# Weight exponents moved by a factor in ScalarE, the clamp replaced by a row sum, and loads chained by issue

## The chip, the cores and the metric

The kernel runs on one core of one Trainium2 chip. The metric is device time in microseconds (us), the median of several runs. A core has a matrix engine (PE), a vector engine (DVE), a scalar engine (ACT), a general engine (POOL) and a queue processor (SP) that here issues nearly all DMAs.

## The reference

A linear attention with decay (4 batches, 8 heads, 768 steps, 48 channels a head) feeds two feed-forward layers (3072 tokens, width 384, inner width 2048). The weights w_in and w_out arrive as 64-bit floats and are converted to 32 bits on the chip.

```
for t in range(S):
    cur = einsum('bhd,bhe->bhde', u[None] * kt, vt)
    y[:, :, t] = einsum('bhd,bhde->bhe', rt, state + cur)
    state = wt[..., None] * state + einsum('bhd,bhe->bhde', kt, vt)
# twice, with weights of their own:
h = maximum(x @ w_in, 0);  x = (h * h) @ w_out
```

## The kernel before

**Tiling.** The attention is cut into 24 tiles of 128 tokens. Each layer walks over blocks of tokens: 512, 256, 256, 512, 512, 512, 512 in the first layer and 512, 512, 512, 512, 512, 256, 256 in the second. Within a block there are 16 slots, one for each chunk of 128 inner channels. A slot is nine matmuls into `h` (L675), relu, square, a rounded copy `gh` and a rest `gl` (L682 to L700), and the matmuls into `acc` (L718). Each fp32 factor is split into a high and a low part (`whi`, `wlo`, `xh`, `xl`, `gh`, `gl`), and three products replace one. From the first matmul of a layer's first block on, chunk f of the weights has to be ready for slot f.

**The weights.** A chunk of weights is loaded as 64-bit numbers (`raw`, 786 KB), and `chunk_ops` (L433) makes fp32 of it in the class `ToFloat32`: `magnitude` on ACT takes the absolute value of the high word (L407). Then four DVE operations on 128x768 numbers follow: `clamp` (L410), `shift` (L413), `top` (L416) and `tail` (L419). ACT copies the result to `whi` (L451) and DVE subtracts that to get `wlo` (L454). There are three `raw` buffers and two `c` buffers, so chunk k+3 can be loaded only when `tail` of chunk k is done. In the first layer the sixteen conversions run beside the ramp and the first block.

**An attention tile.** `wkr` (decays, keys, queries by channel) is loaded by L181, `vn` and `sv` (values) by L192 and L195. DVE runs two scans, G and F (L216, L222), forms a product `rk` (L233) and scales keys and queries by the scans (L246). ACT squares the scans into a sum that is tested at the end (L250). PE, ACT and POOL make scores, masks and states; DVE carries the state (`Sp` L323, `Sn` L333), adds up `ys` (L363) and makes `xl` (L379) beside ACT's `xh`. The first block needs the x of tiles 0 to 3. Until then PE runs matmuls on `ident` only to stay busy (L624).

**What sets the order.** Nothing is scheduled at run time. `Order` keeps a model of time at build: each operation has an engine, a cost from the table `COST`, what it needs, the buffers it takes and gives back, and a due time. `run` picks the operation that can start first, with ties by due time, and writes it out. The engines then execute in that order and wait on semaphores. For a load the model's result counts as there when modelled transfers have been served, plus `LATENCY` (2 us). In the kernel before each load of a kind (`w` for wkr, `v`, `rk`, `raw`) needs the previous one of its kind, that is, its landing in the model. These needs exist in the model alone; on the chip SP issues in the written order, waits for buffers, and each of eight DMA semaphores is reused in turn, so a ninth load waits until the first has landed.

Of the kernel before, what the change touches and what calls it, by code (L numbers as in the profile page):

```python
# [19 lines left out]
T = 128  # L20
# [16 lines left out]
HIGH_WORD_MIN, HIGH_WORD_MAX = 2.0 ** -15, 2.0 ** 16 * (1.875 - 2.0 ** -23)  # L37
RAW_BUFS = 3
# [9 lines left out]
            pe_y=1.14, pe_x=0.45, magnitude=0.91, clamp=0.55, shift=0.56, top=0.96, tail=0.96, hi=0.83, lo=0.96, issue=0.4, warm=0.3)  # L48
# [6 lines left out]
class Order:  # L55
# [37 lines left out]
    def run(self):  # L93
        while self.missing:
# [21 lines left out]
            if gives is not None:  # L116
                self.at[gives], self.by[gives] = end, "DMA" if moves else engine
                for o in self.waiting.pop(gives, ()):
                    o[10] -= 1
                    if not o[10]:  # L120
                        self.ready.append(o)


class Attn:
# [4 lines left out]
    def __init__(self, ctx, tc, wkr, nat, u, ub, ps):  # L129
# [11 lines left out]
        self.chk = cp.tile([QR, NTILE], F32, name="chk")  # L141
# [19 lines left out]
    def tile_ops(self, order, i, due, xdst):  # L161
# [22 lines left out]
        for n, (lo, hi) in enumerate(zip(cuts, cuts[1:])):  # L184
            add("SP", C_["issue"], lambda lo=lo, hi=hi: load_wkr(lo, hi), "w" if n == 0 else f"w{n}", [f"w{n - 1}" if n > 1 else "w"] if n else [("w", i - 1)] if i else [],
# [11 lines left out]
        add("SP", 3 * C_["issue"], load_v, "v", [("v", i - 1)] if i else [], -0.5, take=[("v", i)], moves=8 * T * DM)  # L197

        if not by_pe:
# [4 lines left out]
            add("SP", C_["issue"], load_rk, "rk", [("rk", i - 1) if i > SUMMED_BY_PE else ("rkT", i - 1)], -0.5, take=[("rk", i)], moves=8 * T * DM)  # L204
# [45 lines left out]
        add("ACT", C_["square"], lambda: nc.scalar.activation(out=t["GF"][:, :, 1:], in_=t["GF"][:, :, 1:], func=AF.Square, accum_out=self.chk[:, i:i + 1]),  # L250
# [131 lines left out]
    def out_of_range(self):  # L382
# [39 lines left out]
class Weights:  # L422
# [10 lines left out]
    def chunk_ops(self, order, k, due):  # L433
# [11 lines left out]
        def magnitude():  # L445
            t["conv"] = ToFloat32(nc, t["raw"], self.tmp_p.tile([128, 2 * DM], I32, tag="c", name="c"))
# [158 lines left out]
def chunked(ctx, tc, wkr, nat, u, ub, w1, w2, out):  # L605
# [53 lines left out]
    for k in range(2 * KF):  # L659
        W.chunk_ops(order, k, at[number[k // KF, 0, k % KF]] - 12)  # L660
# [194 lines left out]
```

## Time and profile before

| what | us |
|---|---|
| median of 3 runs (lowest, highest) | 968.42 (965.11, 970.42) |
| profiled execution: its own time | 969.43 |
| profiled execution: span in the trace | 967.6 |
| PE busy | 944.3 (98%) |
| DVE busy | 541.0 (56%) |
| ACT busy | 470.1 (49%) |
| POOL busy | 103.4 (11%) |

Busy PE is not useful PE: matmuls are pipelined, their ends are modelled, and the matmuls on `ident` count as busy. The useful work of the two layers starts with the first L675. A share over the whole span is a mean over a ramp, a first block with conversions, and a long rest, so the stretches are read apart.

### The profile page before, as it was taken

The numbers are of one execution on the slowest core, as the hardware profiler recorded it, in microseconds if no ns is written. First come the engines' busy times: TensorE is split into PE (matmuls) and PEld (weight loads), VectorE is DVE, ScalarE is ACT, GpSimd is POOL, SyncE is SP. The second block draws the span as 40 slices with busy tenths as digits, with TensorE's granted clock in tenths as the row PEclk, the third lists the DMA queues.
The fourth block names the chain that finished last, engine by engine and source line by source line (L and its number), as shares of the span: only waits on it lengthen the run. The fifth ranks groups of instructions, "written<-read, shape, count | busy, mean of one in ns | idle before, by whom it ended". The sixth has DMA issues, their size and how long they took to land.

```text
span 967.6 us, 16982 instructions
## 1 busy us (share of the span) xinstructions
PE 944.3 (98%) x6836; PEld 829.2 (86%) x6836; DVE 541.0 (56%) x946; ACT 470.1 (49%) x875; POOL 103.4 (11%) x122
## 2 busy tenths in 40 slices
PE   9899989999999999999999999999999999999996
PEld 9787678999887878878888889999999999999996
DVE  5889898778756465563337899432322322223332
ACT  3577757566645545464444565432433423333442
POOL 1301113044403123030100000000000000000000
PEclk9799999999999999999999999999999999999999
DMA  8355424154313322131024353110200100100000
GB/s 261 117 160 193 148 78 124 34 141 124 108 33 97 114 70 91 33 96 45 1 73 157 130 179 105 35 43 1 65 1 1 60 1 1 50 1 14 31 18 20
DMA packets 28119, 73.83 MB, mean 76 GB/s; under 512 B 3616, under 2 KB 15264, under 8 KB 28032
## 3 DMA queue, kind: packets, MB, share of 16 engines
q1 hardware_dynamic: 27904, 72.66, 24.2%
q8 instruction: 55, 0.90, 0.4%
q14 instruction: 32, 0.26, 0.1%
q10 hardware_dynamic: 128, 0.00, 0.0%
HBM read 63.21 MB, written 9.44 MB: 75 GB/s over the span
## 4 chain that ended last, share of the span: by engine, by line
PE 89%; DVE 7%; issue 2%; ACT 1%; DMA 1%; POOL 0%; DVEq 0%; POOLq 0%; ACTq 0%
PE acc L718 40%; PE h L675 39%; PE h L624 3%; PE ab L289 2%; PE ab L358 2%; DVE gl L700 1%; PE ab L314 1%; PE ab L258 1%; DVE c L416 1%; DVE Sp L323 1%; PE ab L368 1%; DVE gh L694 1%; DMA wkr<-in_wkr_dram 1%; DVE wlo L454 0%; DVE c L419 0%
## 5 line engine op out<-in xcount | busy, mean ns | idle before, releaser
L682 ACT ACTIVATE gf<-h 128x512 f32<-128x512 f32 (+1 forms) x224 | 120.0, 536 | 350.5 <-PE h L675 345.0
L694 DVE CAST gh<-gf 128x512 fp32r<-128x512 f32 (+1 forms) x208 | 87.3, 420 | 325.8 <-PE acc L718 294.1
L675 PE MATMUL h<-xh,whi 128*128 128x512 f32 (+1 forms) x672 | 245.2, 365 | 0.0
L675 PE MATMUL h<-xh,wlo 128*128 128x512 f32 (+1 forms) x672 | 243.0, 362 | 0.2 <-DVE wlo L454 0.2
L675 PE MATMUL h<-xl,whi 128*128 128x512 f32 (+1 forms) x672 | 242.9, 362 | 0.1
L700 DVE TENSOR_TENSOR gl<-gf,gh 128x512 fp32r<-128x512 f32 (+1 forms) x224 | 144.3, 644 | 15.6 <-ACT gh L694 0.8
L675 PEld LDWEIGHTS h<-xh,wlo 128*128 128x128 f32 x672 | 126.5, 188 | 20.2 <-DVE wlo L454 1.0
L675 PEld LDWEIGHTS h<-xl,whi 128*128 128x128 f32 x672 | 126.6, 188 | 17.5 <-DVE xl L379 0.7
L675 PEld LDWEIGHTS h<-xh,whi 128*128 128x128 f32 x672 | 126.6, 188 | 17.4
L687 ACT ACTIVATE gf<-gf 128x512 f32<-128x512 f32 (+1 forms) x224 | 128.1, 572 | 6.8
L718 PE MATMUL acc<-whi,gl 128*128 128x384 f32 x384 | 129.4, 337 | 0.0
L718 PE MATMUL acc<-whi,gh 128*128 128x384 f32 x384 | 129.3, 337 | 0.0
L718 PE MATMUL acc<-wlo,gh 128*128 128x384 f32 x384 | 128.9, 336 | 0.0
L718 PE MATMUL acc<-gl,whi 128*128 128x512 f32 (+1 forms) x336 | 122.3, 364 | 6.1 <-DVE gl L700 5.3
L718 PE MATMUL acc<-gh,whi 128*128 128x512 f32 (+1 forms) x336 | 124.9, 372 | 0.6 <-DVE gh L694 0.5
L718 PE MATMUL acc<-gh,wlo 128*128 128x512 f32 (+1 forms) x336 | 121.5, 361 | 0.0
L718 PEld LDWEIGHTS acc<-gl,whi 128*128 128x128 f32 x336 | 63.7, 190 | 18.0 <-DVE gl L700 8.2
L718 PEld LDWEIGHTS acc<-whi,gh 128*128 128x128 f32 x384 | 72.3, 188 | 3.5
L718 PEld LDWEIGHTS acc<-wlo,gh 128*128 128x128 f32 x384 | 72.2, 188 | 3.4
L718 PEld LDWEIGHTS acc<-gh,whi 128*128 128x128 f32 x336 | 63.6, 189 | 11.3 <-DVE gh L694 0.7
L718 PEld LDWEIGHTS acc<-whi,gl 128*128 128x128 f32 x384 | 72.0, 188 | 0.0
L718 PEld LDWEIGHTS acc<-gh,wlo 128*128 128x128 f32 x336 | 63.7, 190 | 9.4
(64 smaller groups left out, 946.7 us busy)
## 6 DMA issues: line engine op xcount, KB each, us to landing
raw<-in_w_dram SPq DMA_DIRECT2D x32, 768.0 KB, 4.4
wkr<-in_wkr_dram SPq DMA_DIRECT2D x23, 675.9 KB, 6.7
rk<-in_nat_dram SPq DMA_DIRECT2D x18, 384.0 KB, 5.3
vn<-in_nat_dram SPq DMA_DIRECT2D x24, 192.0 KB, 2.6
sv<-in_nat_dram SPq DMA_DIRECT2D x48, 96.0 KB, 2.6
out_dram<-o SPq DMA_DIRECT2D x24, 192.0 KB, 1.9
x<-o SPq DMA_DIRECT2D x15, 256.0 KB, 2.2
xr<-x SPq DMA_DIRECT2D x12, 256.0 KB, 2.6
```

The source lines that it names most:

```text
L258: nc.tensor.transpose(out=kbv[:, p, :], in_=kS[:, 2 * p:2 * p + 2, :].rearrange("q c t -> q (c t)"), identity=self.ident[0:QR, 0:QR])
L289: nc.tensor.matmul(out=t["sc"][other[a], n, :], lhsT=kS[rows, n, :], rhs=rT[rows, n, :], start=True, stop=True)
L314: nc.tensor.matmul(out=t["U"][c][q, p, :], lhsT=t["ksT"][rows, p, q], rhs=t["vn"][rows, 2 * p + a, :], start=True, stop=True)
L323: nc.vector.tensor_tensor(out=t["Sp"], in0=self.Sc[b], in1=ae, op=ALU.mult)
L358: nc.tensor.matmul(out=y[64 * c:64 * c + 64, D * h:D * h + D], lhsT=t["rs"][rows, a, 2 * p + c, :], rhs=t["sv"][rows, a, 2 * p + c, :], st ...
L624: nc.tensor.matmul(out=t[:, 0:128], lhsT=A.ident, rhs=A.ident, start=True, stop=True)
L675: nc.tensor.matmul(out=h[:, 0:N], lhsT=a[:, cs], rhs=b[:, kk, 0:N], start=n == 0, stop=n == 8)
L682: nc.scalar.activation(out=g[:, 0:N], in_=hs.pop((l, j, f))[:, 0:N], func=AF.Relu)
L687: nc.scalar.activation(out=g[:, 0:N], in_=g[:, 0:N], func=AF.Square)
L694: copy(out=gh[:, 0:N], in_=g[:, 0:N])
L700: nc.vector.tensor_tensor(out=gl[:, 0:N], in0=g[:, 0:N], in1=gh[:, 0:N].bitcast(F32), op=ALU.subtract)
L718: nc.tensor.matmul(out=dst, lhsT=a, rhs=c, start=f == n == 0, stop=f == KF - 1 and n == 2)
```

## The change

**In the conversion.** ACT's magnitude now multiplies the high word by 2^-111 (`SCALE`) and also writes the sum of each row into a column of `chk`, which has 32 columns more and 128 rows. The clamp is gone. `shift` has one operation instead of two, `top` takes one sign bit instead of two bits, `whi` is a copy scaled by 2^-8 (`BACK`), and `wlo` is a scalar_tensor_tensor (c times 2^-8, minus whi) where it was a tensor_tensor. The row sums are compared with 2^-96 (`LARGEST`) in `out_of_range`, together with the attention's sums; this test and its matmul are placed a block later. If it fails, the general path computes everything again, as before.

**In the order.** A load in the model now needs that the previous load of its kind has been issued, not that it has landed. The cost of `magnitude` is 1.1 instead of 0.91.

```
+SCALE, BACK, LARGEST = 2.0 ** -111, 2.0 ** -8, 2.0 ** -96
-  magnitude=0.91, clamp=0.55, shift=0.56, ...
+  magnitude=1.1, shift=0.56, ...
   if moves:
+      self.tell(("issued", gives), end, engine)
       self.dma = max(self.dma, end) + moves / RATE
       end = self.dma + LATENCY
-  add("SP", C_["issue"], load_wkr, ..., [("w", i - 1)], -0.9, ...)
+  add("SP", C_["issue"], load_wkr, ..., [("issued", ("w2" if i == 1 else "w", i - 1))], -0.9, ...)
   (the same for "v" and "rk")
-  t["conv"].magnitude()        # activation(out=cf, in_=high, func=AF.Abs)
+  nc.scalar.activation(out=t["cf"], in_=t["high"].bitcast(F32), func=AF.Abs, scale=SCALE,
+                       accum_out=chk[:, NTILE + k:NTILE + k + 1])
+  shift: nc.vector.tensor_scalar(out=t["c"], in0=t["c"], scalar1=3, scalar2=None, op0=ALU.logical_shift_left)
+  top:   scalar_tensor_tensor(out=c, in0=high, scalar=-0x80000000, in1=c, bitwise_and, bitwise_or)
-  nc.scalar.copy(out=t["hl"][0], in_=t["conv"].cf)
+  nc.scalar.activation(out=t["hl"][0], in_=t["cf"], func=AF.Copy, scale=BACK)
-  nc.vector.tensor_tensor(out=t["hl"][1], in0=t["conv"].cf, in1=t["hl"][0].bitcast(F32), op=ALU.subtract)
+  nc.vector.scalar_tensor_tensor(out=t["hl"][1], in0=t["cf"], scalar=BACK, in1=t["hl"][0].bitcast(F32),
+                                 op0=ALU.mult, op1=ALU.subtract)
-  add("SP", "issue", load, "raw", [("raw", k - 1)] if k else [], take=[("raw", k)], ...)
+  add("SP", "issue", load, "raw", [("issued", ("raw", k - 1))] if k else [], take=[("raw", k)], ...)
-  add("DVE", "clamp", lambda: t["conv"].clamp(), "clamp", ["abs"], port=True)
-  order.add("DVE", 0.5, lambda: next(flag), "rows", last, due=at[number[1, 0, 0]])
+  order.add("DVE", 0.5, lambda: next(flag), "rows", last, due=at[number[1, 1, 0]])   # last: also all ("abs", k)
```

**What stands where now, SP at the program's start.** The piece of 521 columns of `wkr` is tile 0's decays; its two pieces of 512 are tile 0's keys and queries; 1545 columns are a whole later tile. Before:

```order
L181 DMA wkr<-in_wkr_dram 112x521
L192 DMA vn<-in_nat_dram 128x384
L195 DMA sv<-in_nat_dram 64x384 x2
L443 DMA raw<-in_w_dram 128x1536
L156 DMA uB<-in_u_dram 128x384
L181 DMA wkr<-in_wkr_dram 112x512
L181 DMA wkr<-in_wkr_dram 112x1545
L192 DMA vn<-in_nat_dram 128x384
L195 DMA sv<-in_nat_dram 64x384 x2
L443 DMA raw<-in_w_dram 128x1536
L181 DMA wkr<-in_wkr_dram 112x512
```

The same place in the changed kernel:

```order
L188 DMA wkr<-in_wkr_dram 112x521
L188 DMA wkr<-in_wkr_dram 112x512 x2
L188 DMA wkr<-in_wkr_dram 112x1545
L199 DMA vn<-in_nat_dram 128x384
L202 DMA sv<-in_nat_dram 64x384 x2
L199 DMA vn<-in_nat_dram 128x384
L202 DMA sv<-in_nat_dram 64x384 x2
L188 DMA wkr<-in_wkr_dram 112x1545
L451 DMA raw<-in_w_dram 128x1536 x2
L163 DMA uB<-in_u_dram 128x384
L451 DMA raw<-in_w_dram 128x1536
```

Tile 0's three pieces now lead, and the first weights stand behind three tiles' `wkr`.

**DVE near the program's start**, after the scan F of tile 0 (the lines L216 and L222, now L223 and L229, are the scans). Before:

```order
L410 TENSOR_SCALAR c<-c 128x768
L413 TENSOR_SCALAR c<-c 128x768
L416 SCALAR_TENSOR_TENSOR c<-raw,c 128x768
L419 SCALAR_TENSOR_TENSOR c<-raw,c 128x768
L454 TENSOR_TENSOR wlo<-c,whi 128x768
L233 TENSOR_TENSOR rk<-wkr 112x512
L246 TENSOR_TENSOR wkr<-wkr,GF 112x512 x2
L233 TENSOR_TENSOR rk<-wkr 112x512
L410 TENSOR_SCALAR c<-c 128x768
L233 TENSOR_TENSOR rk<-wkr 112x512
L215 MEMSET starts 112x8
L216 SCALAR_TENSOR_TENSOR GF<-wkr,starts 112x520
```

The same place in the changed kernel:

```order
L240 TENSOR_TENSOR rk<-wkr 112x512
L253 TENSOR_TENSOR wkr<-wkr,GF 112x512 x2
L240 TENSOR_TENSOR rk<-wkr 112x512
L222 MEMSET starts 112x8
L223 SCALAR_TENSOR_TENSOR GF<-wkr,starts 112x520
```

The conversion of chunk 0 no longer stands between tile 0's scans and its products; it comes after tile 3's products.

**DVE at the end of the ramp**, up to the `xl` of tile 3, for which the first slot waits. Before:

```order
L379 TENSOR_TENSOR xl<-ab,xh 128x3x128
L416 SCALAR_TENSOR_TENSOR c<-raw,c 128x768
L419 SCALAR_TENSOR_TENSOR c<-raw,c 128x768
L363 TENSOR_TENSOR ys<-ab,vn 128x384
L222 SCALAR_TENSOR_TENSOR GF<-wkr,starts 112x520
L379 TENSOR_TENSOR xl<-ab,xh 128x3x128
L454 TENSOR_TENSOR wlo<-c,whi 128x768
```

The same place in the changed kernel:

```order
L386 TENSOR_TENSOR xl<-ab,xh 128x3x128
L472 SCALAR_TENSOR_TENSOR wlo<-c,whi 128x768
L222 MEMSET starts 112x8
L223 SCALAR_TENSOR_TENSOR GF<-wkr,starts 112x520
L225 TENSOR_SCALAR aend<-GF 112x8
L226 RECIPROCAL starts<-aend 112x8
L370 TENSOR_TENSOR ys<-ab,vn 128x384
L459 TENSOR_SCALAR c<-c 128x768
L462 SCALAR_TENSOR_TENSOR c<-raw,c 128x768
L386 TENSOR_TENSOR xl<-ab,xh 128x3x128
L465 SCALAR_TENSOR_TENSOR c<-raw,c 128x768
L229 SCALAR_TENSOR_TENSOR GF<-wkr,starts 112x520
```

Tile 4's scan G now stands ahead of tile 3's `ys` (its second half F behind the last `xl`), and `tail` of chunk 2 has moved behind the last `xl` as well. From the second block of the first layer on, the matmuls stand in PE's queue at the same slots as before, but for a few moved by one slot.

## Rows read from the trace of the kernel before

**Rows 1.** The page's first part: PE's busy time, share, count; then the other engines.

```profile
PE 944.3 (98%) x6836; PEld 829.2 (86%) x6836; DVE 541.0 (56%) x946; ACT 470.1 (49%) x875; POOL 103.4 (11%) x122
```

**Rows 2.** Windows by stage: length, busy PE, PEld, DVE, ACT, POOL, granted clock, DMA share, GB/s.

```profile
0.00:61.90 61.90, 55.43 (x648) 51.81 (x648) 45.12 (x75) 28.83 (x52) 13.27 (x22) 0.89 0.58 172
61.90:143.70 81.80, 75.49 (x492) 59.22 (x493) 77.49 (x109) 58.11 (x94) 10.66 (x10) 0.98 0.47 153
143.70:500.00 356.30, 353.02 (x3284) 299.71 (x3283) 220.77 (x412) 198.67 (x401) 79.52 (x90) 1.00 0.27 78
500.00:967.60 467.60, 460.35 (x2417) 418.46 (x2415) 197.60 (x352) 184.52 (x329) 0.00 (x0) 1.00 0.15 49
```

**Rows 3.** Waits of PE, 61.9 to 143.7 us: total, times, longest.

```profile
PE acc L718 <- DVE gl L700: 5.3, 5, 2.1
```

**Rows 4.** Timeline of PE at 109 us: start, duration, what, idle before and its releaser.

```profile
109.83 0.68 PE L718 MATMUL acc<-gl,whi 128*128 128x512 f32 x1 [2.06 <-DVE gl L700]
```

**Rows 5.** Windows of 5 us behind that stall.

```profile
110.00:115.00 5.00, 5.00 (x16) 3.90 (x17) 4.90 (x8) 2.90 (x5) 0.00 (x0) 0.66 0.55 170
```

**Rows 6.** Timeline of the first 22 us: DVE, ACT and SP.

```profile
3.93 1.24 DVE L216 TENSOR_TENSOR_SCAN GF<-wkr,starts 112x520 f32<-112x520 f32 x1 [2.30 <-DMA wkr<-in_wkr_dram]
5.65 1.24 DVE L222 TENSOR_TENSOR_SCAN GF<-wkr,starts 112x520 f32<-112x520 f32 x1
...
7.72 1.79 SPq L181 DMA_DIRECT2D wkr<-in_wkr_dram  x2
7.72 0.90 ACT L407 ACTIVATE c<-raw 128x768 f32<-128x768 f32 x1 [5.16 <-DMA raw<-in_w_dram]
...
17.38 0.69 DVE L233 TENSOR_TENSOR rk<-wkr 112x512 f32<-112x512 f32 x1 [3.72 <-DMA wkr<-in_wkr_dram]
18.11 1.29 DVE L246 TENSOR_TENSOR wkr<-wkr,GF 112x512 f32<-112x512 f32 x2
...
19.43 1.07 ACT L250 ACTIVATE GF<-GF 112x1040 f32<-112x1040 f32 x1 [2.05 <-DVE wkr L246]
...
20.41 0.18 ACT L250 ACTIVATION_READ_ACCUMULATOR GF<-GF 112x1 f32 x1
...
21.83 1.24 DVE L216 TENSOR_TENSOR_SCAN GF<-wkr,starts 112x520 f32<-112x520 f32 x1
```

**Rows 7.** Timeline at the end of the ramp: DVE, then PE's first full matmuls.

```profile
51.26 0.46 DVE L323 TENSOR_TENSOR Sp<-Sn,aend 112x192 f32<-112x192 f32 x1 [0.98 <-ACT sv L326]
...
54.39 0.36 DVE L333 TENSOR_TENSOR Sn<-ab,Sp 112x192 f32<-112x192 f32 x1 [1.04 <-PE ab L314]
55.53 0.56 DVE L363 TENSOR_TENSOR ys<-ab,vn 128x384 f32<-128x384 f32 x1 [0.79 <-PE ab L358]
...
61.27 0.56 DVE L379 TENSOR_TENSOR xl<-ab,xh 128x384 fp32r<-128x384 f32 x1
...
61.88 0.50 PE L675 MATMUL h<-xl,whi 128*128 128x512 f32 x1
```

**Rows 8.** DVE by line and form, 61.5 to 147 us: count, busy, mean ns, idle before.

```profile
L419 DVE SCALAR_TENSOR_TENSOR c<-raw,c 128x768 int32<-128x768 int32 x13 | 14.1, 1082 | 0.4
L454 DVE TENSOR_TENSOR wlo<-c,whi 128x768 fp32r<-128x768 f32 x14 | 13.3, 949 | 2.4 <-ACT whi L451 2.3
L416 DVE SCALAR_TENSOR_TENSOR c<-raw,c 128x768 int32<-128x768 int32 x13 | 12.8, 984 | 0.5
...
L410 DVE TENSOR_SCALAR c<-c 128x768 f32<-128x768 f32 x13 | 7.6, 584 | 0.0
L413 DVE TENSOR_SCALAR c<-c 128x768 int32<-128x768 int32 x13 | 7.2, 557 | 0.3
L246 DVE TENSOR_TENSOR wkr<-wkr,GF 112x512 f32<-112x512 f32 x6 | 3.8, 680 | 0.0
...
L222 DVE TENSOR_TENSOR_SCAN GF<-wkr,starts 112x520 f32<-112x520 f32 x2 | 2.5, 1234 | 0.0
```

**Rows 9.** Timeline of DVE at 200 us, in the third block.

```profile
200.44 1.24 DVE L216 TENSOR_TENSOR_SCAN GF<-wkr,starts 112x520 f32<-112x520 f32 x1 [0.68 <-DMA wkr<-in_wkr_dram]
```

More of the change, by code (lines that the diff above doesn't have):

```diff
@@ L47 @@
             ys=0.56, xh=0.48, xl=0.56, natural=1.0, reduce=0.55, bonus=0.83, zero=0.25, pe_ksT=0.55, pe_q=0.96, pe_scores=1.15, pe_u=0.26,
-            pe_y=1.14, pe_x=0.45, magnitude=0.91, clamp=0.55, shift=0.56, top=0.96, tail=0.96, hi=0.83, lo=0.96, issue=0.4, warm=0.3)
+            pe_y=1.14, pe_x=0.45, magnitude=1.1, shift=0.56, top=0.96, tail=0.96, hi=0.83, lo=0.96, issue=0.4, warm=0.3)
 HOP, LATENCY, RATE = 0.07, 2.0, 290e3
@@ L115, in run, with tell @@
                 self.pools[p][2][key] = end
[L116 to L121, printed above, removed]
+            self.tell(gives, end, "DMA" if moves else engine)
+    def tell(self, event, t, by):
+        self.at[event], self.by[event] = t, by
+        for o in self.waiting.pop(event, ()):
+            o[10] -= 1
+            if not o[10]:
+                self.ready.append(o)
 class Attn:
@@ L195, in load_v @@
                 nc.sync.dma_start(out=t["sv"][rows, a], in_=self.nat_d[i, rows, 3].rearrange("t (n e) -> t n e", n=SEG))
[L197 removed]
+        add("SP", 3 * C_["issue"], load_v, "v", [("issued", ("v", i - 1))] if i else [], -0.5, take=[("v", i)], moves=8 * T * DM)
         if not by_pe:
@@ L453, in lo @@
         def lo():
-            nc.vector.tensor_tensor(out=t["hl"][1], in0=t["conv"].cf, in1=t["hl"][0].bitcast(F32), op=ALU.subtract)
-        add("SP", "issue", load, "raw", [("raw", k - 1)] if k else [], take=[("raw", k)], moves=2048 * DM)
+            nc.vector.scalar_tensor_tensor(out=t["hl"][1], in0=t["cf"], scalar=BACK, in1=t["hl"][0].bitcast(F32), op0=ALU.mult, op1=ALU.subtract)
+        add("SP", "issue", load, "raw", [("issued", ("raw", k - 1))] if k else [], take=[("raw", k)], moves=2048 * DM)
@@ L457, in chunk_ops @@
         add("ACT", "magnitude", magnitude, "abs", ["raw"] + ([("abs", k - 1)] if k else []), take=[("c", k)])
-        add("DVE", "clamp", lambda: t["conv"].clamp(), "clamp", ["abs"], port=True)
-        add("DVE", "shift", lambda: t["conv"].shift(), "shift", ["clamp"], port=True)
-        add("DVE", "top", lambda: t["conv"].top(), "top", ["shift"], port=True)
-        add("DVE", "tail", lambda: t["conv"].tail(), "tail", ["top"], port=True, drop=[("raw", k)])
+        add("DVE", "shift", shift, "shift", ["abs"], port=True)
@@ L462, in chunk_ops @@
+        add("DVE", "top", top, "top", ["shift"], port=True)
+        add("DVE", "tail", tail, "tail", ["top"], port=True, drop=[("raw", k)])
         add("ACT", "hi", hi, "whi", ["tail"] + ([("whi", k - 1)] if k else []), take=[("w", k)])
@@ L798, in chunked @@
     bad = []
-    last = [("chk", i) for i in range(NTILE)] + [("x", i) for i in range(NTILE)]
-    order.add("DVE", 0.5, lambda: next(flag), "rows", last, due=at[number[1, 0, 0]])
-    order.add("PE", 0.2, lambda: bad.append(next(flag)), "bad", ["rows"], take=[("ab", "bad")], drop=[("ab", "bad")], due=at[number[1, 0, 2]])
+    last = [("chk", i) for i in range(NTILE)] + [("x", i) for i in range(NTILE)] + [("abs", k) for k in range(2 * KF)]
+    order.add("DVE", 0.5, lambda: next(flag), "rows", last, due=at[number[1, 1, 0]])
+    order.add("PE", 0.2, lambda: bad.append(next(flag)), "bad", ["rows"], take=[("ab", "bad")], drop=[("ab", "bad")], due=at[number[1, 1, 2]])
     order.idle = keep_warm
```

30 lines of the change are left out of this document (20 added, 10 removed).

## The prediction, made before the changed kernel ran

> **What bounds the kernel now.** I read PE's busy share first [rows 1]: 98%. PE can hardly be the thing to relieve, unless part of its work is not useful. So I cut the span into stages [rows 2] and looked at what PE does in each. From 143.7 us to the end it is busy 813.4 of 823.9 us at full clock. The change touches no matmul there, and only idle time could be won. Up to 61.9 us PE is busy 55.4 us, but the first matmul of a slot that runs through starts at 61.88 [rows 7]; what stands before is attention of four tiles and filling matmuls. This ramp is set by a chain through DVE, ACT and the loads. Between the two lies the first block, 61.9 to 143.7 us: DVE is busy 77.5 of 81.8 us and PE 75.5, so PE lacks 6.3 us, and nearly all of it is one wait, for `gl` from DVE [rows 3]. After the longest of these waits, 2.06 us [rows 4], the granted clock of the next window is 0.66, a stretch at 1.2 GHz instead of 2.4 [rows 5]; over the block the mean is 0.98, so some 1.6 us (0.02 x 81.8) go there too.
>
> So two things can be won: the length of the ramp, and about 7.9 us in the first block.
>
> **The ramp.** In the rows of the start [rows 6], tile 0's second scan starts at 5.65 us and takes 1.24, so its products could begin at 6.9. They begin at 17.38, after a wait of 3.72 us for a piece of `wkr`. That piece is one of the two issued from 7.72 on, behind weights, values and all of tile 1's `wkr`. Between the landing of the first weights (ACT starts on them at 7.72) and that of this piece, at 17.38, stand 2.53 MB by the shapes in SP's order: uB 0.20, wkr 0.23, wkr 0.69, values 0.39, raw 0.79, wkr 0.23. That is 262 KB/us, and they arrive in the order of issue.
>
> In the changed order tile 0's pieces lead. The first lands before 3.93, as now [rows 6]; 0.46 MB more at 262 KB/us land at 5.7, tile 1's `wkr` (0.69 MB) at 8.3. DVE reaches the products of tile 0 at 6.9 and `rk` of tile 1 at 6.9 + 0.73 + 1.29 = 8.9 (17.38 to 18.11 is one product with its gap). Both loads are there. Then the scan of tile 1 waits for ACT's square of tile 0: products end at 8.9, square and read of the accumulator take 1.17 (19.43 to 20.41 plus 0.18), so the scan starts at about 10.25. It stands at 21.83 now: **11.6 us earlier**. I need nothing from the weights here, whose landings come out at 17 to 23 us (three raws of 0.79 MB behind two tiles' values and the third `wkr`), while the first DVE operation on them stands behind tile 3's products, at about 34 us.
>
> From there on, DVE does nearly the same work up to tile 3's `xl`: chunk 0's `shift`, `top`, `tail` and `wlo` come in, three clamps, one `tail` and one F scan go out. Much of this stretch is no DVE work at all but the tiles' own chain: `Sp` at 51.26 waits for ACT, `Sn` at 54.39 and `ys` at 55.53 for PE [rows 7]. I take it as shifted by 11.6, so that `Sp` stands at 39.66. From `Sp` to the end of `xl` it is 10.57 us now (51.26 to 61.83). In the new order I add up DVE's row in that piece: `Sp` and `Sn` three times 0.4 to 0.46 and 0.36 (2.3), `ys` and `xl` two each at 0.56 (2.2), `wlo` twice 0.95 (1.9), `tail` 0.96, G of tile 4 with its two small operations 1.7 (3.93 to 5.65), `shift` 0.56, `top` 0.98, together 10.6, and the two waits for PE of 1.04 and 0.79 stay: 12.4. So `xl` ends at 52.05, against 61.83. **The ramp gets 9.8 us shorter.** Bounds: the products of tile 1 share no time with POOL's work in the new order and may run faster, and PE's filling may end earlier, 12 us; if ACT's added pieces (`whi` of chunk 1 and the fourth magnitude now stand ahead of tile 3's `xh`) are late, 8.
>
> **The first block.** Per chunk the clamp goes, 584 ns [rows 8], thirteen of them: 7.6 us of DVE. `tail` of chunk 2 (1.08) and F of tile 4 (1.23) come into the block, two products of 0.68 leave it [rows 8]. DVE's work goes from 77.5 to 77.5 - 7.6 + 2.3 - 1.4 = 70.8 us. PE's own work is 75.5 less the 1.6 of slow clock, 73.9. So PE becomes the bound, by 3 us. It won't be free of waits: the order puts `tail` 2, F, `wlo` 4 and the two new products of tiles 4 and 5 ahead of the third `gl`, and PE's queue has tile 5's transposes there, which I make about 1.3 us late; later, small ones. I allow 3 us of waits with no fall of the clock: the block takes 76.9 instead of 81.8, **4.9 us less**. Bounds: 0 (new waits eat all) and 7.9 (no wait left).
>
> **The edits that cost.** The accumulator's read is 0.18 us [rows 6], thirteen times 2.4 us on ACT in the block, which is busy 58.1 of 81.8 [rows 2]: hidden, and if its cover went, the price would be those 2.4. No row shows ACT's magnitude or copy with a factor; the nearest is the same call without one, 0.90 [rows 6], and I take it for both. `shift` with one operation: 557 ns with two [rows 8], kept. `wlo` as scalar_tensor_tensor has no row of its own; the nearest are `top` and `tail`, the same instruction on the same 768 numbers, 984 and 1082 ns beside 949 for the present tensor_tensor [rows 8]. I take 0.96 and no cost; the upper end is twice the present price. The chunks of layer two are converted after 500 us, where DVE is busy 197.6 of 467.6 us [rows 2]: nothing won or lost. The test and its matmul are a handful of instructions in that stage.
>
> The Trainium skill says otherwise on `wlo`: in Vector Engine (DVE) Microarchitecture Reference, section Points that are easy to get wrong, a scalar_tensor_tensor with two sources in SBUF that are not bf16 has half the throughput. `top` and `tail` have two such sources and run at the tensor_tensor's rate within 14%, so by the rows it does not bite here.
>
> **The sum.** 9.8 + 4.9 = 14.7 us. Against the profiled execution, 967.6 of span and 1.8 around it: 969.4 - 14.7 = 954.7. The median of the runs is 1.0 lower, so **954** (968.4 - 14.7 = 953.7).
>
> **The rivals.**
>
> *Only the ramp* (the waits for `gl` come back in another shape, since DVE and PE are within 3 us of each other): 968.4 - 9.8 = 958.6. For it speaks that in the block three engines hand each slot around; against it that 7.6 us of DVE work do go.
>
> *The loads share the engines* instead of arriving in order of issue: then tile 0's pieces land with what is issued beside them, 2.2 MB up to the second tile's values, at 3.9 + 1.94/0.262 = 11.3. The ramp gains 4.4 less: 958. The 262 KB/us worked out above speak against it.
>
> *Everything is won*: 12 + 7.9 gives 948.5. Three engines without a wait are not likely.
>
> *`wlo` at half rate* (what the page's rule above would make): 14 times 0.95 more in the block put DVE at 84.1 us, longer than PE by far; with the 4.3 us that DVE idles now the block takes 88.4, 6.6 more than before, and two such operations in the ramp's last piece cost 1.9. 968.4 - 9.8 + 1.9 + 6.6 = 967: no change.
>
> *Slower: late tiles at the block boundaries.* With loads tied to issue, `rk` is written ahead of `wkr` for nearly every tile, and `wkr` waits in SP's queue behind the buffer of `rk`. One scan waits for `wkr` now, 0.68 us [rows 9]. If tiles came late at the six later boundaries of layer one, each could cost what the worst wait costs: 2.06 us and 1.7 of slow clock (5 us at 0.66) [rows 4, 5], 3.8 each, 22.6 together: 976. It decides from the fourth boundary on (14.7/3.8). Against it: PE's queue is the same slot by slot there, and x stands in it a slot or more ahead of its block.
>
> *It doesn't do what it says*: the row test fails on good weights and the general path runs. 768 numbers below 2^-110 sum to less than 2^-100, against 2^-96, so I give it 0.01; it would be far slower.
>
> **How the numbers follow.** Chances: forecast 0.55, only the ramp 0.18, sharing loads 0.11, everything 0.06, half rate 0.05, late tiles 0.04, failed test 0.01. The range, 949 to 961.5, takes in the forecast with its bounds on both sides (8 for the ramp and nothing in the block would be 960.4) and leaves out half rate, late tiles and the edges. About 0.5%, 4.8 us, is what a measurement of this kernel can tell from no change; faster by more is all above 963.6: the first four cases, 0.90, less 0.02 for their tails. Same: half rate and such tails, 0.07. Slower: 0.05.
>
> **What would show it.** The product of tile 0 at about 7 us and the second scan G at about 10; the first full matmul of a slot at 52 (50 to 54); the window of the first block with DVE at some 71 us and PE's waits for `gl` at 3 us or less; `wlo` near 0.96; clock 1.00 in the block; from the second block on, the same length to the end, 824 us. It would be wrong if the first product stood at 11, if `wlo` took 1.9, or if PE waited for `gl` as long as now.

## The result and the profile after

The changed kernel takes 952.2 us (median of 4 runs, 950.6 to 952.7), against 967.9 us for the kernel before in the same series (965.1 to 970.4): a ratio of 0.983, with an interval of 0.9814 to 0.9847. Forecast were 954 and a range of 949 to 961.5. The execution that was profiled took 952.65 us, with a span of 950.9; the one of before had a span of 967.6, so 16.7 us have to be found.

The page's first part for the changed kernel. The 60 matmuls that are fewer [rows 1] are filling ones of the shorter ramp (142 on `ident` where there were 202).

```profile
span 950.9 us, 16872 instructions
...
PE 931.3 (98%) x6776; PEld 819.6 (86%) x6776; DVE 527.7 (55%) x915; ACT 472.1 (50%) x907; POOL 109.4 (12%) x123
```

Windows of the changed kernel, cut where they were cut before: at the first matmul of a slot that runs through, at the first one of width 256 (the second block), and at the end. Columns as in [rows 2].

```profile
0.00:53.28 53.28, 45.92 (x588) 42.40 (x588) 41.97 (x70) 28.32 (x55) 14.07 (x23) 0.87 0.73 198
53.28:130.44 77.16, 74.19 (x498) 60.55 (x498) 71.98 (x98) 60.57 (x109) 12.08 (x10) 0.98 0.50 163
130.44:950.90 820.46, 811.19 (x5693) 716.62 (x5691) 413.74 (x749) 383.22 (x744) 83.23 (x90) 1.00 0.20 62
```

Against [rows 2] the ramp went from 61.9 to 53.3 us (8.6 less), the first block from 81.8 to 77.2 (4.6 less), the rest from 823.9 (the last two rows there) to 820.5 (3.5 less). A part of this is the place of the cut: in the changed kernel six matmuls into `acc` (129.08 to 130.44 us, 1.4 us) stand ahead of the first one of width 256, and before they stood behind it. Cut alike, the block takes 75.8 us (6.0 less) and the rest 821.8 (2.1 less). The waits of PE in the first block are now these (total, times, longest):

```profile
PE ab L265 <- ACT rs L299: 2.5, 1, 2.5
PE acc L735 <- DVE gl L717: 0.5, 1, 0.5
```

The five waits for `gl`, 5.3 us in all [rows 3], shrank to one of 0.5. A single other wait has come in, for ACT's copy of tile 4's scores. The timeline shows its place and what follows (start, duration, instruction, idle time before it and its releaser):

```profile
68.75 0.58 ACT L299 COPY rs<-ab 64x512 f32<-64x512 f32 x1
69.36 0.84 ACT L469 ACTIVATE whi<-c 128x768 fp32r<-128x768 f32 x1
70.22 0.58 ACT L299 COPY rs<-ab 64x512 f32<-64x512 f32 x1
...
70.86 0.60 PE L265 MATMUL ab<-ident,wkr 112*128 112x112 f32 x4 [2.46 <-ACT rs L299]
...
72.89 0.39 PE L692 MATMUL h<-xh,whi 128*128 128x512 f32 x1
...
73.85 0.63 PE L692 MATMUL h<-xh,whi 128*128 128x512 f32 x1
```

Chunk 4's `whi` stands between the two copies; PE gets the bank of the scores only after the second, and then runs at the lower of its two clock levels for a while: a matmul of 0.39 us takes 0.63, and from 73.2 to 76.6 us the granted clock is 0.50. This is the same pair as in [rows 4, 5], one wait and one stretch at 1.2 GHz, with another releaser. (That the second follows from the first is not shown: e5_nosum below has the wait without the stretch.)

The start of the run, DVE, ACT and POOL:

```profile
6.86 0.67 DVE L240 TENSOR_TENSOR rk<-wkr 112x512 f32<-112x512 f32 x1
7.56 1.30 DVE L253 TENSOR_TENSOR wkr<-wkr,GF 112x512 f32<-112x512 f32 x2
8.94 1.28 ACT L257 ACT_TABLE_LOAD   x1 [8.94 <-DVE wkr L253]
...
10.25 0.69 DVE L240 TENSOR_TENSOR rk<-wkr 112x512 f32<-112x512 f32 x1 [1.39 <-DMA wkr<-in_wkr_dram]
...
11.43 1.24 DVE L223 TENSOR_TENSOR_SCAN GF<-wkr,starts 112x520 f32<-112x520 f32 x1 [0.47 <-ACT GF L257]
...
13.64 2.26 POOL L303 TENSOR_SCALAR_AFFINE_SELECT rs<-rs 64x512 f32<-64x512 f32 x2 [11.13 <-ACT rs L299]
14.31 2.94 DVE L253 TENSOR_TENSOR wkr<-wkr,GF 112x512 f32<-112x512 f32 x2
```

Tile 0's product starts at 6.86 instead of 17.38 [rows 6], the second scan at 11.43 instead of 21.83. Two rows of the kernel before belong beside these, ACT's table load (the load of the tables for its functions) and the two products of tile 1:

```profile
1.28 1.28 ACT L407 ACT_TABLE_LOAD   x1 [1.28 <-PEq L845]
...
25.02 2.47 DVE L246 TENSOR_TENSOR wkr<-wkr,GF 112x512 f32<-112x512 f32 x2
```

DVE by line and form in the changed kernel, 52 to 131 us (count, busy, mean ns, idle before):

```profile
L462 DVE SCALAR_TENSOR_TENSOR c<-raw,c 128x768 int32<-128x768 int32 x14 | 15.2, 1086 | 0.3
...
L472 DVE SCALAR_TENSOR_TENSOR wlo<-c,whi 128x768 fp32r<-128x768 f32 x14 | 13.3, 952 | 3.0 <-ACT whi L469 2.6
...
L459 DVE TENSOR_SCALAR c<-c 128x768 int32<-128x768 int32 x13 | 7.2, 551 | 0.0
```

The clamp's row [rows 8] is gone, `shift` costs the same with one operation as with two (551 and 557 ns), and `wlo` is as long as before (952 and 949).

### The profile page after: what moved, and what is told of

Its sections match the earlier page's. It is cut to its first block, busy times and chain, and to the rows that moved or that the text cites. A ratio compares the mean times of both kernels' runs of the same rounds, so it can differ in the third digit from the quotient of the medians.

```text
span 950.9 us, 16872 instructions
## 1 busy us (share of the span) xinstructions
PE 931.3 (98%) x6776; PEld 819.6 (86%) x6776; DVE 527.7 (55%) x915; ACT 472.1 (50%) x907; POOL 109.4 (12%) x123
## 4 chain that ended last, share of the span: by engine, by line
PE 76%; DVE 0%; ACT 0%; issue 0%
PE acc L735 36%; PE h L692 36%; PE ab L365 2%; PE ab L296 1%; PE ab L321 1%; PE ab L265 1%; PE ab L375 0%; DVE GF L223 0%; DVE gh L711 0%; DVE aend L225 0%; ACT o L742 0%; DVE gl L717 0%; PE ab L400 0%; DVE starts L226 0%
## 5 line engine op out<-in xcount | busy, mean ns | idle before, releaser
L711 DVE CAST gh<-gf 128x512 fp32r<-128x512 f32 (+1 forms) x208 | 85.2, 409 | 331.3 <-PE acc L735 295.9
L735 PE MATMUL acc<-whi,gh 128*128 128x384 f32 x384 | 129.3, 337 | 0.0
L735 PE MATMUL acc<-wlo,gh 128*128 128x384 f32 x384 | 128.9, 336 | 0.0
L303 POOL TENSOR_SCALAR_AFFINE_SELECT rs<-rs 64x512 f32<-64x512 f32 x48 | 38.1, 794 | 296.8 <-ACT rs L299 295.3
```

What stands on the lines that cost most here:

```text
L303: nc.gpsimd.affine_select(out=x, in_=x, pattern=[[0, SEG], [1, C]], base=0, channel_multiplier=-1, compare_op=ALU.is_gt, fill=0.0)
L711: copy(out=gh[:, 0:N], in_=g[:, 0:N])
L735: nc.tensor.matmul(out=dst, lhsT=a, rhs=c, start=f == n == 0, stop=f == KF - 1 and n == 2)
```

## The experiments

The first theory was that of the prediction: two gains that add up, one by the loads and one by the conversion. All times below are of one profiled execution each, split at the same three places; "end of block" is ramp and first block together. Ratios go to runs of the kernel before on the same chip. The kernels were measured on several chips, so ratios compare better than medians.

| kernel | median us | ratio and interval | ramp | block | rest | end of block |
|---|---|---|---|---|---|---|
| before | 967.9 | | 61.9 | 81.8 | 823.9 | 143.7 |
| changed | 952.2 | 0.983 (0.9814 to 0.9847) | 53.3 | 77.2 | 820.5 | 130.4 |
| e1_issue | 970.7 | 1.0014 (0.9993 to 1.0036) | 54.4 | 85.4 | 829.4 | 139.8 |
| e2_convert | 966.1 | 0.996 (0.9933 to 0.9988) | 62.9 | 73.6 | 827.5 | 136.5 |
| e3_clamp | 968.1 | 0.9992 (0.9971 to 1.0013) | 51.6 | 85.9 | 828.3 | 137.5 |
| e10_half | 961.4 | 0.9925 (0.9895 to 0.9954) | 52.9 | 81.0 | 825.6 | 133.9 |
| e9_clamp_late | 953.7 | 0.9841 (0.9811 to 0.987) | 53.6 | 78.7 | 822.6 | 132.3 |
| e13_issue_noclamp | 953.9 | 0.9816 (0.9779 to 0.9853) | 51.6 | 77.7 | 823.6 | 129.3 |
| e12_notail | 949.2 | 0.9789 (0.9767 to 0.9811) | 54.3 | 71.1 | 823.6 | 125.4 |
| e4_table | 951.5 | 0.9818 (0.9789 to 0.9848) | 52.1 | 77.2 | 819.3 | 129.3 |
| e8_whi_after | 951.1 | 0.9822 (0.9791 to 0.9852) | 52.8 | 76.2 | 820.6 | 128.9 |
| e5_nosum | 951.9 | 0.9815 (0.9792 to 0.9838) | 54.9 | 76.0 | 821.7 | 130.9 |
| e6_values | 953.1 | 0.9834 (0.9805 to 0.9863) | 54.8 | 74.3 | 822.5 | 129.1 |
| e11_both | 951.1 | 0.9818 (0.9793 to 0.9843) | 53.0 | 76.2 | 820.2 | 129.2 |

The changed kernel, e9_clamp_late, e4_table, e8_whi_after, e5_nosum and e11_both have the six `acc` matmuls ahead of the second cut. To compare them with the other rows, take 1.4 us from their block and end of block and add it to their rest.

### The loads alone

In the kernel before, the chains of loads only (the same for `wkr`, the values and `rk`):

```diff
-        add("SP", "issue", load, "raw", [("raw", k - 1)] if k else [], take=[("raw", k)], moves=2048 * DM)
+        add("SP", "issue", load, "raw", [("issued", ("raw", k - 1))] if k else [], take=[("raw", k)], moves=2048 * DM)
```

> The kernel before with one part of the change: every chain of loads tied to issue instead of landing; the conversion keeps clamp, tensor_tensor and plain magnitude. Theory A (two separate gains: the loads' order shortens the ramp, the smaller DVE work the first block): first product at 6.9 us, first full matmul of a slot at 54 to 55 (53.3 as in the changed kernel plus two or three clamps of 0.58), the first block 81 to 83 us long with PE's waits for gl at 4 us or more, total 958 to 961. Theory B (the loads alone made the whole gain): 952. Theory C (the conversion alone): 968, first product at 17.

The ramp came as expected, 54.4 us, and yet the kernel is no faster: 970.7. Theory A's total is refuted. Windows of e1_issue, then PE's waits in its first block:

```profile
0.00:54.41 54.41, 47.34 (x598) 44.51 (x598) 42.91 (x72) 28.30 (x51) 13.85 (x22) 0.87 0.69 193
54.41:139.76 85.35, 77.68 (x491) 61.15 (x492) 80.71 (x112) 59.11 (x95) 10.64 (x10) 0.94 0.44 148
139.76:969.20 829.44, 814.97 (x5699) 719.67 (x5697) 425.64 (x764) 383.65 (x729) 83.62 (x90) 1.00 0.19 61
```

```profile
PE acc L721 <- DVE gl L703: 4.2, 3, 2.1
PE ab L261 <- DVE wkr L249: 2.9, 1, 2.9
PE h L678 <- DVE wlo L457: 0.5, 2, 0.3
```

DVE did 45.1 us of work in the ramp and 77.5 in the first block before [rows 2], 122.6 together; here it is 42.9 and 80.7, 123.6. The work is the same, the ramp is shorter, and what found room in the ramp's idle time is now done in the block, where DVE is busy 80.7 of 85.4 us. PE waits 7.6 us and the granted clock falls to 0.94 in the mean. Of 7.5 us won in the ramp 3.6 go back at once. Another 5.5 go in the rest, and that is not DVE's lack of room in the first block: PE's waits for `Sn`, `gh` and `gl` there are 6.9 us instead of 3.1, scattered from 161 to 426 us.

### The conversion alone

The changed kernel, with all chains of loads as they were before (the chain of the weights is shown, the others go alike):

```diff
-        add("SP", "issue", load, "raw", [("issued", ("raw", k - 1))] if k else [], take=[("raw", k)], moves=2048 * DM)
+        add("SP", "issue", load, "raw", [("raw", k - 1)] if k else [], take=[("raw", k)], moves=2048 * DM)
```

> The changed kernel with the other part alone: the conversion without clamp, with factor, row sums and test, but every chain of loads tied to landing, as before. Theory A: first product at 17.4, first full matmul at 60 to 62, first block 76 to 78 us with DVE at 71 to 72, total 961 to 964; the gains of this run and of e1_issue together make that of the change (15.7). Theory B: 968. Theory C: 952.

Ramp 62.9, block 73.6, below the expected 76 to 78; total 966.1, longer than the expected 961 to 964. Windows of e2_convert, and PE's two largest waits behind its first block (136.5 to 549 us):

```profile
62.87:136.47 73.60, 71.84 (x492) 58.27 (x492) 68.00 (x93) 58.20 (x104) 10.50 (x10) 1.00 0.49 160
136.47:964.00 827.53, 813.67 (x5699) 718.54 (x5697) 416.05 (x749) 385.13 (x745) 81.30 (x90) 1.00 0.20 61
```

```profile
PE ab L321 <- DVE Sn L340: 3.7, 4, 1.7
PE acc L735 <- DVE gh L711: 2.4, 1, 2.4
```

The block gains 8.2 us, and 3.6 of that is lost behind it, where the waits are 6.1 us instead of 3.1 before and 1.5 in the changed kernel. The two parts alone are worth nothing and 0.4%; together 1.7%. Up to the end of the first block most of it adds up: 3.9 (143.7 to 139.8) and 7.2 (to 136.5) are 11.1, of 13.2 (to 130.4), or of 14.6 when cut alike. The larger part of what does not add up lies in the rest: 5.5 and 3.6 us longer alone, 3.5 shorter together (2.1 when cut alike).

### The clamps put back

The changed kernel with a clamp for each chunk (its cost in the planner's table, 0.55, is not shown):

```diff
+        def clamp():
+            nc.vector.tensor_scalar(out=t["cf"], in0=t["cf"], scalar1=0.0, scalar2=LARGEST, op0=ALU.max, op1=ALU.min)
-        add("DVE", "shift", shift, "shift", ["abs"], port=True)
+        add("DVE", "clamp", clamp, "clamp", ["abs"], port=True)
+        add("DVE", "shift", shift, "shift", ["clamp"], port=True)
```

> The changed kernel with a clamp of the same form (maximum and minimum, 768 numbers, in place) put back behind each magnitude and its cost put back in the planner; its bounds leave the numbers as they are. Theory A (the clamps' time on DVE is what the first block lost): DVE in the block 78 to 80 us, block 80 to 83 long, waits of PE for gl back at 4 us or more, total 956 to 960. Rival (PE is the bound in the block, DVE's spare 5 us take the clamps in): block 77 to 78, total 952 to 953.5.

968.1: neither 956 to 960 nor 952. Sixteen operations of 587 ns, 9.4 us of DVE work in layer one, take back all of the gain. The window of the first block of e3_clamp, and its waits:

```profile
51.58:137.48 85.90, 78.04 (x492) 61.90 (x492) 80.43 (x112) 60.22 (x107) 11.14 (x10) 0.94 0.44 147
```

```profile
PE acc L739 <- DVE gl L721: 4.0, 3, 2.1
PE ab L265 <- DVE wkr L253: 3.0, 1, 3.0
...
```

This is e1_issue again, by a kernel that has all else of the change. From it came theory D: with the clamps in layer one, DVE bounds the first block, and a shorter ramp is then worth little.

### Clamps in layer two alone, and half a clamp

```diff
+        if k >= KF:
+            add("DVE", "clamp", clamp, "clamp", ["abs"], port=True)
```

> The changed kernel with the clamp of e3_clamp put back for layer two's sixteen chunks alone. Theory D (the first block is bound by DVE as soon as the clamps stand in it; after layer one DVE has room): first matmul of a slot at 52.8 and the first block 77 to 78 us as in the changed kernel, total 951 to 954. Rival E (the clamps cost wherever they stand): 16 times 0.58 = 9.3 us more, 961, with new waits of PE in layer two.

953.7, inside theory D's 951 to 954: where DVE has room, the same number of operations costs 1.5 us at most, which is within the scatter of the runs. (The profiled execution is the slowest of the four, 956.7, with a clock of 0.96 in the block.)

```diff
-            nc.vector.tensor_scalar(out=t["cf"], in0=t["cf"], scalar1=0.0, scalar2=LARGEST, op0=ALU.max, op1=ALU.min)
+            nc.vector.tensor_scalar(out=t["cf"][:, 0:384], in0=t["cf"][:, 0:384], scalar1=0.0, scalar2=LARGEST, op0=ALU.max, op1=ALU.min)
```

> The changed kernel with a clamp on half of the numbers of each chunk (384 of 768; about 0.3 us by the 0.56 of operations on 384 and 768 numbers, less a fixed part). Theory D (DVE bound: the time grows with DVE's work): DVE in the first block 75 to 78 us, block 80 to 84 long, total halfway between the changed kernel and e3_clamp, 957 to 963. Rival F (a threshold: what costs is one place where a row of DVE comes too late for PE, tile 5's products with 2.9 to 3.0 us in the two kernels that have the clamp, and what follows): total near one of the ends, 951 to 954 or 965 to 968.

961.4, inside 957 to 963. The end of the first block falls at 133.9 us, midway between the changed kernel's 130.4 and e3_clamp's 137.5. These three points show no threshold: the time grows with DVE's work. (The planner is told of the clamp's cost, 0.55 or 0.3, so each of these kernels also has its own order on DVE; what the order does by itself was not measured apart.) Window of its first block, and the half clamp's row in it (count, busy, mean ns):

```profile
52.89:133.86 80.97, 75.88 (x491) 60.41 (x492) 76.76 (x111) 59.86 (x107) 11.86 (x10) 0.96 0.47 154
```

```profile
L459 DVE TENSOR_SCALAR c<-c 128x384 f32<-128x384 f32 x13 | 5.0, 387 | 0.1
```

### The loads with the clamps left out, nothing else

In e1_issue:

```diff
-        add("DVE", "clamp", lambda: t["conv"].clamp(), "clamp", ["abs"], port=True)
-        add("DVE", "shift", lambda: t["conv"].shift(), "shift", ["clamp"], port=True)
+        add("DVE", "shift", lambda: t["conv"].shift(), "shift", ["abs"], port=True)
```

> The kernel of e1_issue with the clamps left out and nothing else of the conversion changed: no factor, no row sums, the old tensor_tensor, and no test of the weights' range, which is what this kernel leaves out of the computation. Theory D (what the conversion brings is the clamps' time on DVE, and it only counts together with the loads): first matmul of a slot at 52 to 53.5, first block 76 to 78, total 950 to 953. Rival (one of the other edits, a cheaper shift or the test, brings part of it): 955 or more.

953.9 (four runs, 947.0 to 954.7), 0.9 above theory D's 950 to 953 and 1.1 below the rival's 955, so neither range holds it; but by its ratio, 0.9816 beside 0.983, it gains all that the change gains. The factor, the row sums, the new form of `wlo` and the test bring no time that can be measured (953.9 to 952.2 is under 0.5%); leaving the clamp out is what counts, and they are what allows it. Windows of this kernel:

```profile
0.00:51.64 51.64, 45.02 (x585) 42.04 (x585) 41.14 (x69) 28.10 (x51) 13.71 (x22) 0.90 0.71 203
51.64:129.33 77.69, 74.59 (x492) 60.58 (x492) 72.27 (x99) 59.02 (x95) 13.16 (x10) 0.96 0.49 162
129.33:952.90 823.57, 813.40 (x5699) 718.15 (x5697) 417.78 (x748) 382.87 (x729) 85.02 (x90) 1.00 0.20 62
```

### One more operation off DVE

```diff
-        add("DVE", "top", top, "top", ["shift"], port=True)
-        add("DVE", "tail", tail, "tail", ["top"], port=True, drop=[("raw", k)])
+        add("DVE", "top", top, "top", ["shift"], port=True, drop=[("raw", k)])
```

> The changed kernel with one more DVE operation per chunk left out, the one that brings in the low word (0.96 us each; the weights lose their lowest bits). Theory D (with the clamps gone PE is the bound of the first block; what is left to win is its idle time and slow clock, 4.7 us in the block and 1.6 in the later blocks): DVE in the block 58 to 62 us, block 73 to 76, total 946 to 951. Rival J (DVE still sets the block): 13 us less, 939.

This leaves out `tail`, which brings in the low word. 949.2, inside theory D's 946 to 951, with a block of 71.1, below its 73 to 76. DVE has 9.9 us less to do in the block, the block is 6.0 shorter (4.7 when cut alike), and the total only 3.0: PE is the bound of the block now, and in this profile the ramp is 1.0 longer and the rest 1.8, cut alike. Window of the first block of e12_notail:

```profile
54.29:125.42 71.13, 71.13 (x491) 58.49 (x492) 62.12 (x89) 60.19 (x109) 11.86 (x10) 1.00 0.52 169
```

PE doesn't idle for a moment, at full clock. So 71.1 us is what its 491 matmuls of this block take.

### The table load, the place of `whi`, the row sums

```diff
     def load_u(self):
         self.nc.scalar.dma_start(out=self.ub, in_=self.ub_d)
+        self.nc.scalar.activation(out=self.one[:, 0:1], in_=self.one[:, 1:2], func=AF.Square)
```

(The tile `one` and its memset are not shown.)

> The changed kernel with one more activation on a tile of one number, right behind ACT's first load, so that ACT's table is loaded at the start and not at 8.94 us ahead of the first square. Theory A (tile 1's wkr lands at 10.2 and holds DVE's product of r and k, so most of the 1.28 us is hidden by that): the first square ends at about 10.1, the second scan G starts at 10.95 instead of 11.43, first full matmul at 52.8, total 0.5 us less. Rival (the table load is the whole delay of the second scan against my 10.25): G at 10.2, first full matmul at 52.0, total 1.3 us less. Second rival (something later sets the ramp): first full matmul stays at 53.3, total unchanged.

The timeline of ACT in e4_table:

```profile
1.28 1.28 ACT L163 ACT_TABLE_LOAD   x1 [1.28 <-PEq L865]
...
9.20 1.07 ACT L260 ACTIVATE GF<-GF 112x1040 f32<-112x1040 f32 x1 [6.42 <-DVE wkr L256]
...
11.34 0.54 ACT L281 COPY ksT<-ab 128x456 f32<-128x456 f32 x1 [0.97 <-PE ab L271]
```

The second scan moved from 11.43 to 10.98, as theory A said, since DVE waits for tile 1's `wkr` anyway, and ACT's next copy waits for PE until 11.34 (11.30 in the changed kernel). The ramp is 1.2 us shorter in this profile, but kernels whose ramp has the changed kernel's order (53.3 us, granted clock 0.87) have 52.8 (e8_whi_after, clock 0.90) and 54.9 (e5_nosum, clock 0.84) there. So a shorter ramp is not shown, only the 0.45 us at the scan; the median, 951.5, is 0.7 below the changed kernel's, less than its runs scatter.

```diff
-        add("ACT", "hi", hi, "whi", ["tail"] + ([("whi", k - 1)] if k else []), take=[("w", k)])
+        add("ACT", "hi", hi, "whi", ["tail"] + ([("cross1", 4)] if k == 4 else []) + ([("whi", k - 1)] if k else []), take=[("w", k)])
```

> The changed kernel with chunk 4's whi tied to the second copy of tile 4's scores, so that on ACT it stands behind that copy and not between the two. Theory G (the 2.46 us wait of PE at 70.9 for that copy, and the slow clock right behind it, are what is left to win in the first block): the wait falls by whi's 0.85 to 1.6 or less, the block from 77.6 to 75.5 (if the clock stays up) or 76.8, total 950 to 951.5. Rival (chunk 4's wlo comes later and PE waits for it instead): block 77 to 78, total 952.

The wait fell by `whi`'s length, and the clock stayed up. Window of the first block of e8_whi_after, and its waits:

```profile
52.75:128.93 76.18, 73.50 (x498) 59.15 (x498) 71.88 (x98) 60.78 (x109) 12.77 (x10) 1.00 0.50 165
```

```profile
PE ab L265 <- ACT rs L299: 1.6, 1, 1.6
PE acc L735 <- DVE gl L717: 1.1, 2, 0.6
```

The block is 1.0 us shorter, less than the 2.1 of theory G's better case: a second wait for `gl` has come, 0.6, and PE is busy for 73.5 us at full clock, where it was 72.5 (74.2 less the 1.7 of slow clock). Median 951.1. Whether the clock stayed up because the wait is shorter is left open by the next run.

```diff
-            nc.scalar.activation(out=t["cf"], in_=t["high"].bitcast(F32), func=AF.Abs, scale=SCALE, accum_out=chk[:, NTILE + k:NTILE + k + 1])
+            nc.scalar.activation(out=t["cf"], in_=t["high"].bitcast(F32), func=AF.Abs, scale=SCALE)
```

> The changed kernel with the magnitudes' row sums left out (the test reads zeros for them, so it no longer covers the weights); cost in the planner and so the order unchanged. Theory (the reads of the accumulator, 0.18 to 0.20 each, lie beside other work): total 951 to 953. Rival (ACT is now close enough to its limit in the first block, 60.6 of 77.6 us, with the wait for its score copy in it): the wait at 70.9 shrinks by 0.4 or more, total 949.5 to 951.

951.9, and PE's wait for the score copy is 2.5 us as in the changed kernel: the reads of the accumulator are hidden. Window of the first block of e5_nosum, and that wait:

```profile
54.90:130.93 76.03, 72.97 (x498) 59.31 (x498) 71.90 (x98) 59.66 (x97) 11.38 (x10) 1.00 0.51 165
```

```profile
PE ab L265 <- ACT rs L299: 2.5, 1, 2.5
```

Here the clock did not fall behind the same wait, and the block is 1.1 us shorter than the changed kernel's with every wait as long as there. So a slow stretch does not follow each such wait, and the 1.0 us of e8_whi_after can't be put down to the place of `whi`; what that edit shows is a wait 0.9 us shorter.

> The changed kernel with both small edits, the early table load of e4_table and chunk 4's whi behind the second score copy of e8_whi_after. If they add up (0.5 to 1.2 us of ramp, 1.0 of the first block): first matmul of a slot at 51.6 to 52.3, first block 76.7, total 950 to 950.8. If the measured gains were scatter: 952.

This kernel has the edits of e4_table and e8_whi_after. 951.1 (949.3 to 954.3). The first block keeps e8_whi_after's 76.2 us, but the ramp is 53.0, and the total isn't below 950.8. Apart from e12_notail, which leaves out work, no version here beats the changed kernel by more than its runs scatter.

### An edit that did not do what it was meant to

The first of four such edits (the others put tile 2's `wkr`, the weights and `uB` behind these values):

```diff
-        add("SP", 3 * C_["issue"], load_v, "v", [("issued", ("v", i - 1))] if i else [], -0.5, take=[("v", i)], moves=8 * T * DM)
+        add("SP", 3 * C_["issue"], load_v, "v", [("issued", ("v", i - 1))] if i else [("w", 1)], -0.5, take=[("v", i)], moves=8 * T * DM)
```

> The changed kernel with the values of tiles 0 and 1, and all loads behind them, tied to the landing of tile 1's wkr, in the same order on SP. Theory H (loads that are under way together share the engines: the values took 1.9 us from tile 1's wkr, which landed at 10.2 and not at 8.3): product of r and k of tile 1 at 8.9 or before; the second scan stays at 11.4, held by ACT's table load; total 951 to 953.5, later if the values now come too late for tile 0. Rival I (they arrive in order of issue, only slower than 262 KB/us): that product stays at 10.2.

The timeline of SP in e6_values shows the values issued as soon as ever:

```profile
0.82 1.82 SPq L188 DMA_DIRECT2D wkr<-in_wkr_dram  x4
2.69 0.43 SPq L199 DMA_DIRECT2D vn<-in_nat_dram  x1
```

An entry in the planner's list of needs changes the order that the planner writes out; it puts no wait on the chip. So nothing was held back, the product stood at 10.47, and the run tells neither theory from the other. It also says how the change itself is to be read: the need for a landing that it takes out of the model was no wait on the chip, and what differs is the order of issue. (SP does wait for landings where a semaphore is reused: in the changed kernel the first weights, its twelfth load, are issued at 10.24 us, after 3.0 us of waiting for the fourth, tile 1's `wkr`.) What the run was to tell, the changed kernel's DMA records tell in part. Windows 6 to 8 and 8 to 10.2 us, in this order:

```profile
DMA packets 177, 0.50 MB, mean 250 GB/s; under 512 B 21, under 2 KB 121, under 8 KB 177
...
DMA packets 342, 0.50 MB, mean 229 GB/s; under 512 B 54, under 2 KB 329, under 8 KB 342
```

By the shapes a row of tile 1's `wkr` is a packet of 6180 bytes and a row of values one of 1536. From 6 to 8 us, with tile 1's `wkr` under way, 100 packets (121 less 21) are already values, which were issued behind it, and from 8 to 10.2 some 275 of 342 (329 less 54) are. So in these windows loads do share the DMA engines, and a landing does not follow from the bytes ahead of it alone. That the engines don't keep step, and that a load lands when the slowest of them is done with it, would fit, but these records name no engine; nor do they show how much of the 1.9 us from 8.3 to 10.2 the sharing makes.

## Why the prediction was right, and where it was not

**The total** was 2.0 us off the profiled execution (14.7 us forecast, 16.7 found) and 1.8 off the median. Cut alike, the ramp won 1.2 us less than forecast and the block 1.1 more; that these two cancel is luck. What remains is the rest of the run, 2.1 us, which was taken as unchanged.

**The ramp**, 9.8 forecast with bounds of 8 and 12, measured 8.6. Tile 0's product at 6.9 was right (6.86). Three steps behind it failed. Tile 1's `wkr` was to land at 8.3 by 262 KB/us in order of issue; DVE got it at 10.25, by the DMA records above. The rival of shared engines names what these records show, but for the wrong load: tile 0's pieces led and were not delayed. The second scan, forecast at 10.25, stood at 11.43: ACT's table load of 1.28 us had run before at 1.28 us, hidden by the wait for `raw` (ACT's first activation stands at 7.72 in [rows 6]), and now stood ahead of the first square. I had looked at the rows that ACT waits for and not at what it does once. Of the 1.2 us, 0.45 are shown to be the table's (e4_table); without it tile 1's `wkr` holds DVE. And tile 1's products were to share no time with POOL's work and perhaps run faster; they took 2.94 us beside POOL's selects, where they had taken 2.47. So `Sp` stood at 41.24 instead of 39.66, 1.2 us of it by the scan and some 0.5 by the products. The last piece, 12.4 forecast, took 12.0 (41.24 to 53.22).

**The first block**, 76.9 forecast, 77.2 measured, 75.8 when cut alike: near, but for reasons that partly cancel. DVE's work was 72.0 instead of 70.8. PE's waits were 3.0 as allowed, but 2.5 of them for ACT and not for `gl`; ACT's work I had put down as hidden by its share of busy time, which says nothing about an instruction that stands between two others. The clock was not 1.00 but 0.98, with a stretch like that of [rows 5] at a new place (1.7 us); in e5_nosum, with the same order, it was 1.00. And PE's own work is not the 73.9 us of the prediction: e12_notail does it in 71.1 (its block has 491 matmul records, before's 492). A busy PE contains short waits, since a matmul is shown as 0.39 us and the next one starts 0.23 later; a wait of up to 0.16 between two leaves no gap in the record. With this the block adds up: 71.1 of work, 3.0 of waits and 1.7 of slow clock are 75.8. The term that was mis-sized is PE's own work, 73.9 instead of 71.1, and the slow clock, put at nothing, makes up for 1.7 of these 2.8.

**The rest**, taken as unchanged, is 3.5 us shorter. Six matmuls fall before the boundary instead of behind it (498 and 492 in the block), which is 1.4 us; 2.1 are left, and PE's waits there are 1.6 less (3.1 to 1.5). The experiments show that this term is not small: 5.5 us longer in e1_issue, 3.6 in e2_convert, with waits of up to 2.4 us for `gh`, `gl` and `Sn` that lie elsewhere in each order. Which rows of DVE make them late in each was not settled. One row goes along with it: POOL's 36 selects behind the block take 682 ns each in the changed kernel and 723 before, but 806, 839 and 857 in e2_convert, e3_clamp and e1_issue, the three with the longest rest. Whether DVE and POOL hold each other up there was not tested.

**The sum of independent terms** is the step of the argument that was wrong, though its result was right. The rival of the ramp alone, 958.6, let the block keep its 81.8 us. Measured, the ramp alone (e1_issue) gives 970.7. DVE's work up to the end of the first block is a fixed amount (122.6 us before, 123.6 in e1_issue), and a ramp that ends earlier moves it into a block that has no room. That accounts for the block's 3.6 us; the 5.5 behind it, the larger part of the loss, stay open as said above. Only when the clamps go (114.0 us in the changed kernel) is the shorter ramp worth its length: e13_issue_noclamp, which has just these two, comes to 51.6, 77.7 and 823.6. That is 10.3, 4.1 and 0.3 us less, 14.7 in all, the sum that was forecast (one execution, the slowest of its four).

**The costs** came out as taken. `wlo` took 952 ns, as a tensor_tensor does. The Trainium skill's Vector Engine (DVE) Microarchitecture Reference, section Points that are easy to get wrong, gives such an instruction half the throughput. Beside the tensor_tensor's 949 ns the trace doesn't bear that out, and the measurement decides. The accumulator's reads are hidden (e5_nosum). Layer two takes sixteen more DVE operations without a cost that shows (e9_clamp_late). The general path did not run, and no row shows late tiles at the boundaries.

## What to carry to other kernels

Before you add up the gain of a shorter start and that of a lighter engine, sum the busy time of that engine up to the next point where it catches up: if the work is the same and the window shorter, the gain of the start is eaten there, and the two edits are worth much only together. Take an operation off an engine in the stage where that engine sets the time, since the same operation elsewhere showed no cost here. And where an order is planned, price an edit together with the order that it makes: e1_issue, e2_convert and e3_clamp were each 3 to 6 us longer than the kernel before behind the first block, where their edits changed no work of PE.

## What the runs showed of the hardware

Two products of DVE that take 1.30 us took 2.94 while POOL's two selects ran (7.56 and 14.31 us in the changed kernel), 1.64 more; the selects overlapped them for 1.59 (14.31 to 15.90; POOL's spans are rough). In e1_issue and e3_clamp tile 5's pair takes 3.0 us, and PE waits 2.9 to 3.0 for it. The Trainium skill's SBUF — State Buffer, section SBUF: two separate sides, has the two engines take a shared pair of ports in turn, each for a whole instruction; the numbers agree with that.

ACT's table load of 1.28 us is done at 1.28 us when the first activation is one on raw weights (before) or on a constant (e4_table), and only at 8.94 when the first one is the square of what DVE has made: there it waits with its activation.
